# Gated linear attention with a gated feed-forward on one core: the second chunk's phase summed on TensorE, one copy out of PSUM for the turned q and k, and a new order on all engines

## The chip, the core and the metric

The kernel runs on one core of one Trainium2 chip. Its engines are TensorE (PE in the profile; PEld is its weight load), VectorE (DVE), ScalarE (ACT), GpSimd (POOL) and SyncE (SP, which here only starts transfers). Each engine works through its own list of instructions in order, and waits on semaphores where it needs the result of another one. The metric is the device time of the whole program in microseconds, the median of a few runs.

## The reference

Two stages follow one another. The first is a recurrence over 768 tokens for 4 batches of 8 heads with head size 48: a complex state of 48 x 48 per head is multiplied by a complex gate of magnitude below 1 at every token, gains the outer product of k and v, and is read by q. The second is a feed-forward over the 3072 tokens with 384 features.

```python
mag = np.sqrt(a_re * a_re + a_im * a_im)
scale = np.minimum(mag, 0.999) / (mag + 1e-06)
a_re_n, a_im_n = (a_re * scale, a_im * scale)
for t in range(S):                      # S = 768; (B, H, D) = (4, 8, 48)
    new_re = ar * S_re - ai * S_im      # ar, ai: the gate of token t
    new_im = ar * S_im + ai * S_re
    S_re, S_im = (new_re + kv, new_im)  # kv: k outer v of token t
    y[:, :, t] = np.einsum('bhd,bhde->bhe', q[:, :, t], S_re)
# x = y as (3072, 384)
gelu = 0.5 * g * (1.0 + erf(g * inv_sqrt2))       # g = x @ w_gate
ffn_out = gelu * val @ w_out                      # val = x @ w_val, d_ff = 1536
return x + res_gate * ffn_out                     # res_gate = sigmoid(x @ w_res)
```

## The kernel before

**Tiling.** The tokens are cut into 12 groups. Group p holds 256 tokens of batch p % 4 (groups 0 to 3 the first 256 tokens of each batch, 4 to 7 the next, 8 to 11 the last), as two chunks of 128 tokens; a chunk is a tile of 128 tokens by 384 features. The feed-forward runs over 8 units: units 0 to 3 are groups 0 to 3, units 4 to 7 are two groups each.

**Steps.** Every piece of work is a named step; the number is the group or unit, then the chunk or part. For group p:

- Lar, Lai, Lq, Lk, Lvf load a chunk of an input (SP queue). VC casts v.
- SQI, SQR, ADD, LNR, EXR, TH, LM, ATN make the logarithm of the gate's magnitude and its angle (ScalarE and VectorE).
- CSL and CST are TensorE products in float32 with a triangular matrix: they sum the logarithms (line 609) and the angles (line 643) along a chunk's tokens. EX and EI are exponentials of CSL's result. OFF and FR take the whole turns off CST's result; ABS, SIN and COS follow.
- QE, KE (line 705) and QR, KR (line 713) multiply q and k with the magnitude and the turned phase, giving padQ and padK of 96 rows per head.
- q and k are then turned so that the 96 features lie on the partitions. For groups 0 to 4 TensorE does it: TP (line 745) writes 4 heads of q and 4 of k into one PSUM tile of 1024 columns, and two CP steps (line 751) copy 512 columns each to SBUF. For groups 5 to 11 a transposing transfer does it (QT, KT, line 718).
- AT (line 759), AM (762), DK (767), Y (807 and 810), X (818) are attention within the chunk, the causal mask, the state's gain, the output and its copy out of PSUM. EN, EB, MI, ED, and DR, DS, DE, DI, DT, MM, MN bring the state G and its decay from group to group; the D steps are small transfers on POOL's queue.

For unit u: XT and XC, or the transposing transfer XD, turn the attention's output; GP and VP (line 848) are the two up-projections, GE the gelu, HM the product (859), RP and SG the residual gate, OP (873) the down-projection, OT (878), RX (885) and ST the end. The weights (Wg, Wv, Wr, Wo; lines 920 to 926) are loaded with a cast by POOL's queue in 12 pieces; HOLDW and HOLDO are one-element copies on POOL that wait for a given load before later weight pieces are started.

**The carried row.** An angle sum has to go on from chunk to chunk. For groups 4 to 11, after FR of a chunk, CRA (chunk 0 to chunk 1 of the same group) or CRB (chunk 1 to chunk 0 of the next group of that batch), line 688, scales the last 32 rows of the chunk's phase into spare rows of the state tile G, and CDA or CDB (line 693), a transfer that adds, puts its last row onto the first row of the next chunk's angles. CST of the next chunk waits for that. Groups 0 to 3 count chunk 0's angles back from its end and need no carry inside the group.

**What sets the order.** The list ORDER, written out by hand or program, gives all 1,391 steps in one sequence; each engine gets its steps in that sequence. The words log, trig and gelu in it load ScalarE's tables. The dictionary 'eo' says on which engine a step runs where it has a choice. Buffers are taken in turn from rings: four PSUM tiles for CSL, CST, OP, RP, GP, VP, TP and XT, two for AT, one each for Y and DK.

Of the kernel before, what the change touches and what calls it, by code (L numbers as in the profile page):

```python
# [53 lines left out]
 'cpe': ('ACT', 'DVE'),  # L54
# [8 lines left out]
 'cma': [],  # L63
 'xdma': 5,
 'eo': {'CP0.0.0.0': 'ACT',
        'CP0.0.0.1': 'DVE',
        'CP0.0.1.0': 'ACT',
        'CP0.0.1.1': 'DVE',
        'CP0.1.0.0': 'DVE',
        'CP0.1.0.1': 'DVE',  # L70
        'CP0.1.1.0': 'ACT',
        'CP0.1.1.1': 'DVE',
        'CP1.0.0.0': 'DVE',
        'CP1.0.0.1': 'DVE',
        'CP1.0.1.0': 'DVE',
        'CP1.0.1.1': 'ACT',
        'CP1.1.0.0': 'DVE',
        'CP1.1.0.1': 'DVE',
        'CP1.1.1.0': 'ACT',
        'CP1.1.1.1': 'DVE',  # L80
        'CP2.0.0.0': 'ACT',
        'CP2.0.0.1': 'ACT',
        'CP2.0.1.0': 'ACT',
        'CP2.0.1.1': 'DVE',
        'CP2.1.0.0': 'DVE',
        'CP2.1.0.1': 'DVE',
# [24 lines left out]
        'CRA8': 'DVE',
        'CRA9': 'POOL',
        'CRB0': 'DVE',
        'CRB1': 'POOL',
        'CRB2': 'POOL',
        'CRB3': 'POOL',
        'CRB4': 'POOL',
        'CRB5': 'POOL',
        'CRB6': 'DVE',
        'CRB7': 'DVE',  # L120
        'EB10': 'POOL',
# [4 lines left out]
        'EB7': 'POOL',  # L126
        'EB8': 'POOL',
        'EB9': 'ACT',
        'EN10': 'POOL',
# [4 lines left out]
        'EN7': 'POOL',  # L134
        'EN8': 'DVE',
        'EN9': 'POOL',
        'MM10': 'DVE',
# [5 lines left out]
        'MM8': 'POOL',  # L143
        'MM9': 'DVE',
        'MN10': 'POOL',
        'MN11': 'POOL',
        'MN4': 'POOL',
# [4 lines left out]
        'MN9': 'POOL',  # L152
# [12 lines left out]
        'OFF4.0': 'ACT',  # L165
# [3 lines left out]
        'OFF6.0': 'ACT',  # L169
        'OFF6.1': 'DVE',  # L170
# [4 lines left out]
        'OFF9.0': 'ACT',  # L175
        'OFF9.1': 'DVE',
        'RX0.0': 'POOL',
        'RX0.1': 'POOL',
        'RX1.0': 'POOL',
        'RX1.1': 'POOL',  # L180
# [26 lines left out]
        'SQI3': 'DVE',  # L207
        'SQI4': 'DVE',
# [15 lines left out]
        'SQR7': 'DVE',
        'SQR8': 'ACT',
        'SQR9': 'ACT',
        'VC0.0': 'POOL',
        'VC0.1': 'POOL',
        'VC1.0': 'DVE',
        'VC1.1': 'POOL',  # L230
        'VC10.0': 'POOL',
        'VC10.1': 'ACT',
        'VC11.0': 'POOL',
# [3 lines left out]
        'VC3.0': 'POOL',  # L237
# [7 lines left out]
        'VC7.0': 'DVE',  # L245
        'VC7.1': 'POOL',
        'VC8.0': 'POOL',
        'VC8.1': 'ACT',
        'VC9.0': 'ACT',
        'VC9.1': 'POOL',  # L250
        'X0.0': 'ACT',
        'X0.1': 'ACT',
        'X1.0': 'ACT',
        'X1.1': 'ACT',
        'X10.0': 'ACT',
        'X10.1': 'ACT',
# [24 lines left out]
        'XC3.0': 'DVE',
        'XC3.1': 'DVE',
# [6 lines left out]
Lar0.0 log LNR0.0 SQR0.0 Lai0.0 SQI0.0 ADD0.0 LM0.0 Lar0.1 LNR0.1 EXR0.1 Lai0.1 SQI0.1 TH0.1 SQR0.1 EXR0.0 Lai1.1  # L289
CSL0.0 Lai1.0 SQI1 TH0.0 Lar1.0 trig ATN0.1 ADD0.1 Lar1.1 SQR1 ATN0.0 log LM0.1 CST0.0 ADD1 LM1 EX0.0 CST0.1 CSL0.1  # L290
OFF0.0 FR0.0 OFF0.1 Lk0.0 Lvf0.0 Lq0.1 CSL1.1 EI0.0 LNR1 EX0.1 VC0.0 DE0 EXR1 EI0.1 KE0.0 FR0.1 ABS0.1 TH1 trig COS0.1
SIN0.0 ATN1 SIN0.1 CST1.0 CSL1.0 CST1.1 ABS0.0 COS0.0 Lar3.1 Lai4.1 Lai3.0 Lar3.0 Lai3.1 SQR3 SQI3 ADD3 KR0.0 log
EX1.1 LM3 DE1 EI1.0 LNR3 OFF1.0 EX1.0 EI1.1 Lk0.1 Lq0.0 KE0.1 KR0.1 QE0.0 QR0.0 OFF1.1 Lar2.0 Lar4.0 Lar4.1 Lar2.1
Lk1.1 Lai4.0 Lk1.0 Lai2.1 Lai2.0 Lvf0.1 EXR3 Lq1.1 CRB0 FR1.0 FR1.1 Lq1.0 Lvf1.0 TP0.0.1 Lar5.1 CP0.0.1.0 SQR4 ABS1
QE0.1 CP0.0.1.1 AT0.0.1 TP0.0.0 trig COS1 CP0.0.0.0 SQR2 Wg1 SQI4 QR0.1 CP0.0.0.1 SIN1 SQI2 AT0.0.0 TP0.1.1 TH3
AM0.0.0 ADD4 Lai5.1 CP0.1.1.0 ATN3 CP0.1.1.1 DR4 DK0.0 CSL3.0 TP0.1.0 ADD2 VC0.1 CSL3.1 log LNR2 EI3.1 EX3.1 LM2
Lar5.0 AM0.0.1 MI0 Y0.0 KE1 X0.0 EI3.0 LNR4 EX3.0 CP0.1.0.1 CP0.1.0.0 Lai5.0 AT0.1.1 AT0.1.0 EXR2 CST3.0 KR1 AM0.1.1
AM0.1.0 VC1.0 QE1 XT0.0 CSL2.1 Y0.1 CST3.1 EX2.1 OFF3.0 Wv1 EI2.1 QR1 XC0.0 TP1.0.0 TP1.0.1 X0.1 FR3.0 OFF3.1 XT0.1
DK0.1 HOLDO Wg3 Wg0 EXR4 XC0.1 CP1.0.0.1 CP1.0.1.1 GP0.5 FR3.1 ED0 CP1.0.0.0 Lvf1.1 Wr AT1.0.0 GP0.0 GP0.2 HOLDW CRB1
CP1.0.1.0 gelu GE0.5 GE0.2 Wv3 Wg2 TH4 TH2 SQR5 AT1.0.1 RP0.0 TP1.1.1 SG0.0 GE0.0 RP0.1 SG0.1 Wv2 DE3 Wo2 Wv0 VP0.2  # L300
CP1.1.1.0 TP1.1.0 VP0.5 DE2 DK1.0 AM1.0.0 Wo0 AM1.0.1 Y1.0 Wo1 CP1.1.1.1 trig ATN4 AT1.1.1 HM0.5 CP1.1.0.1 Lk2.0 Lk2.1
AM1.1.1 CP1.1.0.0 ATN2 X1.0 GP0.1 GP0.4 CST2.1 HM0.2 GP0.3 AT1.1.0 gelu GE0.1 GE0.3 GE0.4 MI1 SQI5 ABS3 OFF2.1 log LM4
ADD5 CSL2.0 VC1.1 CST2.0 FR2.1 Lq2.1 VP0.4 VP0.3 AM1.1.0 HM0.4 CDB0 DS4.1 HM0.3 Y1.1 Lq2.0 OFF2.0 EI2.0 EX2.0 Lq3.1
Lq3.0 XT1.0 Lk3.0 LNR5 XC1.0 FR2.0 Lk3.1 DR5 CRB3 X1.1 VP0.1 HM0.1 DK1.1 ED1 VP0.0 XT1.1 HM0.0 OP0.1.0 EXR5 XC1.1 TH5
Lar7.1 trig SIN2 OP0.0.0 SIN3 ABS2 COS2 ATN5 GP1.1 COS3 KE2 OT0.1 KR2 QE2 OT0.0 QR2 DS4.0 Lar6.0 gelu GE1.1 RP1.1
GP1.3 SG1.1 GE1.3 GP1.2 TP2.0.0 GE1.2 TP2.0.1 GP1.4 QE3 QR3 CP2.0.0.0 CP2.0.1.1 KE3 CP2.0.1.0 CP2.0.0.1 KR3 CRB2 GE1.4
GP1.5 GE1.5 RP1.0 GP1.0 Lar7.0 SG1.0 AT2.0.1 AT2.0.0 Lvf2.0 Lai6.1 GE1.0 VP1.2 CSL4.0 AM2.0.1 Lar6.1 DS5.0 DS5.1
TP2.1.1 SQR7 log EX4.0 EI4.0 ML4 HM1.2 Lai6.0 ML5 CP2.1.1.0 AM2.0.0 VC2.0 CP2.1.1.1 CSL4.1 VP1.4 VP1.0 HM1.4 HM1.0
TP2.1.0 CP2.1.0.0 CP2.1.0.1 LM5 SQR6 EX4.1 Lvf3.0 Lvf2.1 Lai7.1 Lai7.0 CDB1 RX0.0 DI4 CST4.0 SQI6 Y2.0 CSL5.0 AT2.1.1
OFF4.0 EI4.1 ADD6 FR4.0 EX5.0 LNR6 ME5 EI5.0 Lq4.0 Lk4.0 ST0.0 DK2.0 AT2.1.0 VP1.1 MI2 AM2.1.1 HM1.1 AM2.1.0 VC2.1  # L310
CSL5.1 VP1.5 X2.0 VP1.3 HM1.5 EX5.1 SQI7 EI5.1 DR6 CRA4 HM1.3 ADD7 CST5.0 LM6 EXR6 ME4 OFF5.0 Y2.1 TP3.0.0 CP3.0.0.1
DK2.1 ED2 FR5.0 CP3.0.0.0 TP3.0.1 CP3.0.1.1 TH6 CP3.0.1.0 LNR7 X2.1 OP1.0.0 XT2.0 EXR7 OT1.0 XC2.0 TH7 CDA4 CST4.1
AT3.0.0 OFF4.1 XT2.1 AT3.0.1 TP3.1.1 trig ATN7 ATN6 VC3.0 DT4.1 DK3.0 AM3.0.0 FR4.1 CP3.1.1.1 OP1.1.0 XC2.1 SIN4 MI3
CP3.1.1.0 ABS4 OT1.1 AM3.0.1 GP2.3 GP2.2 TP3.1.0 DT4.0 DR7 RX0.1 COS4 GP2.5 Lvf3.1 CP3.1.0.1 CP3.1.0.0 MM4 CRA5 VC3.1
DK3.1 Y3.0 gelu GE2.5 GE2.3 AT3.1.1 GP2.4 AT3.1.0 RP2.0 RP2.1 GE2.2 GE2.4 Lq4.1 Lk4.1 SG2.1 KE4 AM3.1.1 ED3 KR4 DE5
AM3.1.0 RX1.0 QE4 CDA5 CST5.1 RX1.1 DI5 OFF5.1 SG2.0 MN4 DE4 Lai8.1 GP2.0 X3.0 GP2.1 Lar9.0 Lai9.0 GE2.0 VP2.5 Lvf4.0
Lar8.1 Lq5.1 Lar9.1 FR5.1 VC4.0 DK4.0 QR4 VP2.3 Y3.1 HM2.5 TP4.0.1 TP4.0.0 SQR9 GE2.1 Lvf5.0 VC5.0 DS6.0 HM2.3 trig
SIN5 CP4.0.1.0 CP4.0.1.1 EN4 CDB2 Lai8.0 Lq9.1 CRB5 CP4.0.0.1 Lq6.1 X3.1 CP4.0.0.0 ABS5 Lai9.1 Lar8.0 VP2.0 HM2.0
XT3.0 VP2.2 AT4.0.1 AT4.0.0 XC3.0 AM4.0.1 Lvf4.1 ST1.0 Lvf8.0 VP2.1 VP2.4 CSL6.0 VC8.0 EB4 CRB4 AM4.0.0 COS5 HM2.1
Y4.0 TP4.1.1 Lk8.0 HM2.2 HM2.4 log EI6.0 EX6.0 SQI9 CST6.0 TP4.1.0 Lq5.0 ST1.1 Lk5.0 QE5 ADD9 CP4.1.0.0 LM7 Lk5.1  # L320
CP4.1.0.1 SQR8 SQI8 LNR9 OP2.1.0 CP4.1.1.1 QR5 CP4.1.1.0 OP2.0.0 CDB3 XT3.1 AT4.1.0 OT2.1 OFF6.0 VC4.1 EXR9 ADD8 XC3.1
# [44 lines left out]
class Steps:  # L366
# [24 lines left out]
def kernel(  # L391
# [590 lines left out]
```

## Time and profile before

| | |
|---|---|
| median of 3 runs | 274.76 us (274.43 to 276.25) |
| profiled execution, its own time | 275.13 us |
| its span, first to last instruction | 273.4 us |
| mean granted TensorE clock | 0.963 |
| PE busy | 234.9 us, 86% of the span |
| DVE busy | 222.7 us, 81% |
| ACT busy | 207.9 us, 76% |
| POOL busy | 114.7 us, 42% |
| read from HBM | 31.33 MB |

The profile gives the busy time of each engine, then the same in 40 slices of the span. A group of instructions is told by its source line, engine and tiles, with the count, the summed busy time and the mean of one; the idle time behind it is what the engine lost just before them, with the work that ended the wait. A window answer gives the busy time of each engine between two moments. The difference of 1.7 us between the execution's own time and its span lies around the program's first and last instruction.

### The profile page before, as it was taken

How to read it: one execution, taken by the hardware profiler on the slowest of the kernel's cores; microseconds unless marked ns; L12 is line 12 of the kernel's file. 1: busy time of each engine (PE TensorE's matmuls, PEld its weight loads, DVE VectorE, ACT ScalarE, POOL GpSimd, SP SyncE). 2: the span in 40 equal slices, each digit the busy share in tenths (PEclk: the TensorE clock that was granted, in tenths of full speed). 3: DMA queues.
4: the chain of work that ended last, by engine and by line, in shares of the span. 5: the costliest groups of instructions: out<-in, count | busy, mean ns of one | idle time of the engine just before them, and what ended most of it. 6: DMA issues, size and time to landing. Idle time of an engine off the chain costs nothing.

```text
span 273.4 us, 5330 instructions
## 1 busy us (share of the span) xinstructions
PE 234.9 (86%) x1913; PEld 148.2 (54%) x1926; DVE 222.7 (81%) x369; ACT 207.9 (76%) x343; POOL 114.7 (42%) x164
## 2 busy tenths in 40 slices
PE   0636777978999899997999999899899889999993
PEld 0313546765867777675744565545556445654451
DVE  1888899698999998995899999778998698634534
ACT  5999997999899899797799798979569763124410
POOL 4001197451437798299464385400751250021001
PEclk9985599999999999998999999999999999999999
DMA  7999999999999789899789938697769937132002
GB/s 149 207 207 191 206 199 186 186 183 173 184 220 181 138 181 196 143 174 167 123 166 190 190 70 158 152 215 138 153 74 185 205 80 158 30 95 80 2 29 86
DMA packets 170714, 41.35 MB, mean 151 GB/s; under 512 B 162624, under 2 KB 170688, under 8 KB 170688
## 3 DMA queue, kind: packets, MB, share of 16 engines
q1 hardware_dynamic: 163200, 37.04, 70.1%
q0 software_dynamic: 7488, 3.97, 11.0%
q8 instruction: 15, 0.25, 0.4%
q14 instruction: 11, 0.09, 0.1%
HBM read 31.33 MB, written 4.76 MB: 132 GB/s over the span
## 4 chain that ended last, share of the span: by engine, by line
PE 45%; DMA 18%; ACT 15%; DVE 10%; issue 6%; POOL 3%; SPq 0%; DVEq 0%; ACTq 0%; POOLq 0%
PE gv L848 22%; PE sums L873 8%; DMA wo<-in_moe_w_out_dram 5%; PE sums L643 4%; PE sums L609 4%; DMA wr<-in_moe_w_res_dram 3%; ACT L949 3%; ACT CS L521 3%; DMA KT<-padK 3%; PE sums L863 2%; ACT m L521 2%; DMA xT<-x 2%; PE at L759 2%; DMA QT<-padQ 2%; DVE kE L705 2%
## 5 line engine op out<-in xcount | busy, mean ns | idle before, releaser
L859 DVE SCALAR_TENSOR_TENSOR h<-h,gv 128x512 bf16<-128x512 bf16 x72 | 47.1, 679 | 15.7 <-PE gv L848 15.5
L521 ACT ACTIVATE h<-gv 128x512 bf16<-128x512 f32 x72 | 41.0, 603 | 22.6 <-PE gv L848 21.9
L848 PE MATMUL gv<-xT,wg 128*128 128x256 bf16 (+1 forms) x284 | 52.7, 325 | 4.6 <-DMA xT<-x 1.6
L848 PE MATMUL gv<-xT,wv 128*128 128x256 bf16 (+1 forms) x279 | 55.1, 326 | 1.0 <-DVE h L859 0.6
L873 PE MATMUL sums<-wo,h 128*128 128x384 bf16 x288 | 49.2, 326 | 2.1 <-DMA wo<-in_moe_w_out_dram 1.1
L949 ACT ACT_TABLE_LOAD x34 | 43.6, 1283 | 1.3 <-PEq L966 0.7
L848 PEld LDWEIGHTS <-wg 128*128 128x128 bf16 x288 | 27.4, 98 | 24.0 <-issue 3.8
L873 PEld LDWEIGHTS <-h 128*128 128x128 bf16 x288 | 27.4, 98 | 20.5 <-issue 2.1
L848 PEld LDWEIGHTS <-wv 128*128 128x128 bf16 x288 | 27.2, 99 | 19.0 <-issue 3.8
L762 DVE TENSOR_TENSOR atm<-at,mask 128x512 bf16<-128x512 f32 x48 | 31.8, 681 | 5.5 <-PE at L759 5.2
L885 POOL TENSOR_TENSOR ot<-ot,x 128x384 f32<-128x384 f32 x14 | 14.2, 1019 | 40.0 <-DVE ot L878 39.9
L521 ACT ACTIVATE ar<-ar 128x768 f32<-128x768 f32 (+1 forms) x28 | 23.1, 833 | 0.0
L878 DVE SCALAR_TENSOR_TENSOR ot<-sg,sums 128x384 f32<-128x384 f32 x24 | 12.9, 547 | 10.2 <-PE sums L873 6.3
L532 POOL CAST v<-vf 128x384 bf16<-128x384 f32 x17 | 11.7, 692 | 21.8 <-DMA vf<-in_v_dram 20.7
L609 PE MATMUL sums<-m,lt 128*128 128x384 f32 x24 | 12.3, 600 | 9.0 <-ACT Ei L521 8.5
L643 PE MATMUL sums<-ai,ut 128*128 128x384 f32 x40 | 18.4, 545 | 0.9 <-DMA ai<-G 0.6
L693 POOL DMA_DIRECT2D ai<-G x16 | 14.1, 880 | 8.4 <-ACT ai L521 5.7
L531 ACT CAST x<-y 128x384 bf16<-128x384 f32 x22 | 10.5, 477 | 7.5 <-issue 5.0
L521 ACT ACTIVATE sg<-sums 128x384 f32<-128x384 f32 x24 | 11.7, 499 | 5.1 <-PE sums L863 5.1
L863 PE MATMUL sums<-wr,xT 128*128 128x384 bf16 x72 | 14.6, 325 | 0.6 <-DMA wr<-in_moe_w_res_dram 0.3
L688 POOL TENSOR_SCALAR G<-m 32x384 f32<-32x384 f32 x10 | 14.0, 1397 | 2.8 <-issue 2.1
L521 ACT ACTIVATE m<-m 96x8 f32<-96x8 f32 (+2 forms) x29 | 12.9, 466 | 2.7 <-DMA d<-m 1.1
(94 smaller groups left out, 466.4 us busy)
## 6 DMA issues: line engine op xcount, KB each, us to landing
ar<-in_a_re_dram SPq DMA_DIRECT2D x24, 192.0 KB, 3.8
ai<-in_a_im_dram SPq DMA_DIRECT2D x24, 192.0 KB, 4.0
k<-in_k_dram SPq DMA_DIRECT2D x24, 192.0 KB, 4.3
vf<-in_v_dram SPq DMA_DIRECT2D x24, 192.0 KB, 3.8
q<-in_q_dram SPq DMA_DIRECT2D x24, 192.0 KB, 4.1
out_dram<-ot SPq DMA_DIRECT2D x24, 192.0 KB, 2.5
wg<-in_moe_w_gate_dram POOLq DMA_DIRECT2D x4, 288.0 KB, 7.8
wv<-in_moe_w_val_dram POOLq DMA_DIRECT2D x4, 288.0 KB, 9.2
```

The source lines that it names most:

```text
L521: return nc.scalar.activation(out=out, in_=in_, func=func, **kw)
L609: st.add("CSL%d.%d" % (p, c), "PE", lambda c=c: nc.tensor.matmul(out=st["csl", (p, c)], lhsT=lmat[c], rhs=part(("m2", p), (c,)), start=Tru ...
L643: return r + [nc.tensor.matmul(out=o, lhsT=tmat[c if s == 0 else 1], rhs=part(("ai", p), (c,)), start=not both, stop=True)]
L688: st.add("CR%s%d" % (nm, p), cre, lambda: eng.tensor_scalar(out=row[96:128], in0=part(("m2", p), (c,))[96:128], scalar1=-2.0 * math.pi, sc ...
L693: st.add("CD%s%d" % (nm, p), "POOL", lambda: nc.gpsimd.dma_start(out=part(("ai", pn), (cn,))[0:1], in_=row[127:128], accum_op=OP.add), r=[ ...
L762: st.add("AM" + sfx, "DVE", lambda: nc.vector.tensor_tensor(out=st["atm", i], in0=st["at", i], in1=mask4, op=OP.mult), r=[("at", i)], w=[( ...
L848: st.add("%sP%d.%d" % (nm.upper(), u, f), "PE", lambda f=f, fs=fs, nm=nm, w=w: [nc.tensor.matmul(out=st[nm + "p", (u, f)][:, j * 256:j * 2 ...
L859: st.add("HM%d.%d" % (u, f), "DVE", lambda f=f, h2=h2: nc.vector.scalar_tensor_tensor(out=h2(), in0=h2(), scalar=0.5, in1=gv(("vp", (u, f) ...
L863: st.add("RP%d.%d" % (u, jj), "PE", lambda jj=jj: [nc.tensor.matmul(out=st["rp", (u, jj)], lhsT=st["xT", u][:, i, jj * 128:(jj + 1) * 128] ...
L873: st.add("OP%d.%d.%d" % (u, jj, hh), "PE", lambda jj=jj, fs=fs: [nc.tensor.matmul(out=st["op", (u, jj)], lhsT=st["h2", u][:, f, jj * 128:( ...
L885: st.add("RX%d.%d" % (u, jj), rese, lambda jj=jj, pc=(p, c), eng=eng: eng.tensor_tensor(out=st["ot", (u, jj)], in0=st["ot", (u, jj)], in1= ...
L949: nc.scalar.preload_act_table_set(tables[nm])
```

## The change

Three things are edited, and the order is written anew.

1. For groups 4 to 11, chunk 1 of CST is two products into the same PSUM tile: a matrix that holds 1/(2 pi) everywhere times chunk 0's angles, and the triangular one times chunk 1's. The constant matrix is one column, broadcast. CRA and CDA are gone (8 each); CRB and CDB stay. CST of chunk 1 now reads the angles of both chunks.
2. The two CP copies of 512 columns become one of 1024, on one engine.
3. Every buffer is now picked by a slot number that stands behind the step's name in ORDER, in place of rings.
4. ORDER has 1,355 steps in another sequence, with 34 table loads as before. By the dictionary 'eo', 8 X copies, 3 VC, 4 RX, 4 EB, 3 MN and a few others go to VectorE, and VectorE gives SQI and SQR (one each) to ScalarE; 3 of CRB run on GpSimd where 5 did.

```diff
- 'cma': [],
+ 'cma': [4, 5, 6, 7, 8, 9, 10, 11],
...
-        omat = singles.tile([128, 128], FP, name="omat")
-        nc.vector.memset(omat, I2PI)
+        om = singles.tile([128, 1], FP, name="om")
+        nc.vector.memset(om, I2PI)
+        omat = om.to_broadcast([128, 128])
...
-                for n, eng in enumerate(PARAMS["cpe"]):
-                    eng = on("CP%s.%d" % (sfx, n), eng)
-                    st.add("CP%s.%d" % (sfx, n), eng, lambda n=n, eng=eng: copy(
-                        eng, st["qk", i][0:DD, n * 512:n * 512 + 512], st["tp", i][0:DD, n * 512:n * 512 + 512]),
-                        r=[("tp", i)], w=[("qk", i, n)])
+                cpe = on("CP" + sfx, "DVE")
+                st.add("CP" + sfx, cpe, lambda cpe=cpe: copy(cpe, st["qk", i][0:DD], st["tp", i][0:DD]),
+                       r=[("tp", i)], w=[("qk", i)])
...
-            pools[tag] = ctx.enter_context(tc.tile_pool(name="p" + tag, bufs=PARAMS["bufs"][tag], **kw))
-    psM = ctx.enter_context(tc.tile_pool(name="psM", bufs=4, space=PSUM))
+            pools[tag] = ctx.enter_context(tc.tile_pool(name="p" + tag, bufs=1, **kw))
+    psM = ctx.enter_context(tc.tile_pool(name="psM", bufs=1, space=PSUM))
...
-    tiles["gp"] = tiles["vp"] = lambda: psM.tile([128, 512], FP, name="gv", **mm)
+    tiles["gp"] = tiles["vp"] = lambda sl: psM.tile([128, 512], FP, name="gv", tag="mm" + next(sl))
```

The code that the first edit switches on stood in the kernel before, unused (lines 636 to 645, `both`). The start of the two sequences up to the weights and the first down-projection, most steps left out:

```
before: ... Wg1 SQI4 QR0.1 ... ADD4 Lai5.1 ... DR4 ... Wv1 ... HOLDO Wg3 Wg0 ... GP0.5 ... Wr ... GP0.0 GP0.2 HOLDW CRB1 ... Wv3 Wg2 ... Wv2 DE3 Wo2 Wv0 VP0.2 ... DE2 ... Wo0 ... Wo1 ... HM0.0 OP0.1.0 ... KE2 ... OP0.0.0
after:  ... HOLDO ... ADD4 CP0.0.1 DR4 ... Wg0 Wg2 Wv3 Wg3 ... Wg1 Wv0 ... Wr ... Wo2 Wv1 GP0.5 ... HOLDW ... Wo0 ... DE2 ... VP0.0 ... VP0.5 ... Wv2 ... VP0.4 VP0.2 VP0.3 VP0.1 HM0.2 HM0.3 HM0.1 HM0.4 DS4.0 DR5 Wo1 KE2 ... OP0.0.0
```

More of the change, by code (lines that the diff above doesn't have):

```diff
@@ L125 @@
         'EB6': 'DVE',
[L126 to L129, printed above, removed]
+        'EB7': 'DVE',
+        'EB8': 'DVE',
+        'EB9': 'DVE',
+        'EN10': 'DVE',
         'EN11': 'POOL',
@@ L151 @@
         'MN8': 'POOL',
-        'MN9': 'POOL',
+        'MN9': 'DVE',
         'OFF0.0': 'DVE',
@@ L164 @@
         'OFF3.1': 'DVE',
-        'OFF4.0': 'ACT',
+        'OFF4.0': 'DVE',
         'OFF4.1': 'ACT',
@@ L236 @@
         'VC2.1': 'POOL',
-        'VC3.0': 'POOL',
+        'VC3.0': 'DVE',
         'VC3.1': 'POOL',
@@ L299 @@
[L299 to L308, printed above, removed]
```

365 lines of the change are left out of this document (178 added, 187 removed).

## The prediction

> **What bounds the kernel now.** I read the page's busy slices first, then the PE line of time for its gaps, then the chain of work, then sums over stages.
>
> The page's slices of the span (first line: totals of the engines):
>
> ```profile
> PE 234.9 (86%) x1913; PEld 148.2 (54%) x1926; DVE 222.7 (81%) x369; ACT 207.9 (76%) x343; POOL 114.7 (42%) x164
> ...
> PE   0636777978999899997999999899899889999993
> ...
> DMA  7999999999999789899789938697769937132002
> ```
>
> PE is thin in the first nine slices (some 64 us) and nearly full after. The line of time of PE around that point:
>
> ```profile
> 61.75 0.82 PE L873 MATMUL sums<-wo,h 128*128 128x384 bf16 x4 [0.89 <-DVE h L859]
> 63.64 3.41 PE L873 MATMUL sums<-wo,h 128*128 128x384 bf16 x20 [1.06 <-DMA wo<-in_moe_w_out_dram]
> ```
>
> The first down-projection waits for VectorE, and four products later for the last piece of wo. In the chain of work:
>
> ```profile
> 33.31 0.54 POOL d L594
> 33.85 0.73 POOL v L532
> 34.58 0.71 POOL wv L920
> ...
> 37.67 9.46 DMA wr<-in_moe_w_res_dram
> ...
> 49.40 14.20 DMA wo<-in_moe_w_out_dram
> 63.60 0.04 issue
> 63.64 1.47 PE sums L873 x8
> ```
>
> So before 63.64 us the transfers decide. The window answer over three stages and the tail (columns: stretch, length, busy PE, PEld, DVE, ACT, POOL, clock, DMA share, GB/s):
>
> ```profile
> 0.00:63.64 63.64, 39.16 (x303) 26.45 (x303) 51.81 (x93) 57.36 (x89) 25.79 (x43) 0.87 1.11 190
> 63.64:221.62 157.98, 149.57 (x1293) 96.62 (x1302) 141.97 (x230) 135.82 (x227) 84.44 (x116) 0.99 0.88 162
> 221.62:269.15 47.53, 46.20 (x320) 25.17 (x322) 27.77 (x46) 14.69 (x28) 4.44 (x6) 1.00 0.25 64
> 269.15:273.40 4.25, 0.00 (x0) 0.00 (x0) 1.14 (x3) 0.00 (x0) 0.00 (x0) 1.00 0.37 139
> ```
>
> DMA share 1.11 in the first stage: the transfer engines are full, at 190 GB/s. From 63.64 us to 269.15 us PE is busy 195.8 of 205.5 us; the 94% and 97% leave 9.7 us. The last 4.25 us are OT, RX and the store behind the last product. **The kernel is a start of 63.6 us bound by transfers and VectorE, then 205.5 us of TensorE, then a tail.**
>
> To count TensorE's work I give each step its issue time from the chain of work: GP or VP (6 products of 256 or 3 of 512 columns) 0.65 us, OP 1.95 (12 products), RP 0.49, CSL or one CST product 0.65, TP 0.45, AT 0.225, a pair of products in Y 0.05, DK 0.2 to 0.37. All steps make 228.5 us; 29.0 lie before the first OP and 199.6 from it on. Four products of that OP (0.65) had run by 63.64 us, so 205.5 us carried 199.0 us of work: **6.6 us of loss**, in gaps of 0.2 to 1.7 us that end on many kinds of work, none often.
>
> **The change, part by part.**
>
> *Second phase product.* Eight CST steps become two products. The nearest row is the same shape in float32: "PE sums L643 x2" takes 0.65 us in the chain (one product is two records). 8 x 0.65 = **+5.2 us on TensorE**. The broadcast stationary matrix is not in the trace; the bounds are 0.16 us a product (bf16, 384 columns: 1.95 / 12) and twice 0.65, so +1.3 to +10.4; I take 5.2, since only the weight's access pattern differs. No other work hides it, because all eight products lie after the first OP, where PE has no room.
>
> *The carry.* Away go 8 CRA (5 on POOL at 1.18 us median, 3 on VectorE at 0.36: -5.9 and -1.1) and 8 CDA (0.88 each to issue, 4.1 us to land: -7.0 on POOL). POOL is busy 42% and waits 39.9 us for OT alone, so its time is worth nothing. The chain FR, CRA, CDA, CST loses some 6 us per group, but on PE only one wait of 0.62 us ends on "DMA ai<-G". I take **-0.6 us**; from 0 to -2. What is late next is CST's own input, the angles from ATN.
>
> *One copy.* 29 CP on VectorE at 412 ns and 11 on ScalarE at 578 become 15 and 5. VectorE's 128x384 copy of the same kind takes 348, so 128 columns cost 64 ns and 1024 columns some 0.67 us (between 0.41 and 0.82); ScalarE's 489 and 578 give 0.93 (between 0.58 and 1.16). VectorE 11.95 to 10.0, ScalarE 6.4 to 4.7. AT starts up to 0.35 us later, as two engines no longer share the copy: 7 us over 20 copies at most, 0 to 1 where PE can't do something else. After 63.64 us PE lost 0.32 us on qk: I take 0.
>
> *Engines.* From the 'eo' lists by the rows: X 8 more on VectorE (0.554 each), RX 4 more (0.588), VC 3 (0.436), EB 4 (0.345), MN 3 (0.24), less CP, CRA, SQI, SQR: VectorE **+6.7 us**, ScalarE -5.6, POOL -26. Where does VectorE's surplus fall? Work ahead of the first OP is 61.5 us in the new order against 55.3 (sums of single durations); from there to KR11 it is 158.2 in both; the rest lies in the last 50 us, where VectorE is half idle. So it can only hurt the start. HM0.4, the last that OP0.0.0 needs, has 57 us of VectorE ahead, against 55 for HM0.0 before: ready at about 61.7 + 2 = 63.7 us.
>
> *Weights.* POOL starts them in order. Before, one wg piece goes at 23.1 us, the other 11 from 34.5 us on, all landed at 63.6: 2.65 us a piece while loads of SP share the transfer engines. Now all 12 stand behind DR4, which waits for ADD4. ADD4 has 23.9 us of VectorE ahead against 25.2 (done at 34.2): 33.0 us, plus 0.5 for DR4 is 33.5, and 12 x 2.65 = 31.8: **65.3 us**. Also VP0.4 to VP0.1 now stand behind Wv2, and Wo1 behind DE2, DS4.0 and DR5 in POOL's queue. Bounds: 61 (VectorE alone, if the loads yield) and 69 (two transfers of 4 us ahead). I take 65. SP starts as many loads before the first OP in both (46 and 45), so no bytes go away.
>
> *Order and slots.* Before the first OP of the new order lie 29.6 us of TensorE work, nearly the same 29.0; from it on 204.1 against 199.6. The new order thus puts no added work into the idle start. Its loss after the start is unknown: 0 to 14 us by the rows (6.6 now, twice that); I keep 6.6 less 0.6. Slots fix a buffer but cost no instruction. SP's list holds the same loads and stores; a late XD or QT holds what stands behind it, as now (waits up to 5.5 us there, 1.7 on PE).
>
> **The sum.** 65.0 (start) + 204.1 (TensorE) + 6.0 (loss) + 4.25 (tail) = 279.35 us of span, against 63.6 + 199.0 + 6.6 + 4.25 = 273.4. The execution's own time was 1.73 us above its span: 281.1. The median shown lies 0.37 below that execution: **280.7 us**, 2.2% more.
>
> *A rule beside it.* In the windows of ten microseconds the granted clock is 0.86 from 120 to 130 us and 0.97 in the next ten, around PE's wait of 1.73 us for the turned k, and 0.50 from 20 to 30. The Trainium skill's "TensorE: Matmul & The Clock Gate", section "HAM oscillation", says that idle gaps beyond about 3.4 us bring the half clock back; here a shorter gap preceded it. By that rule a long wait before VP0.4 or OP0.0.0 would add some 1.7 us (half of 3.4, an estimate from that page) and give 282.4.
>
> **Rivals.**
>
> *A. The sum holds* (start 64 to 66, loss 4 to 8): 277.7 to 283.7.
>
> *B. The weights are late.* Place: VP0.4 behind Wv2, OP0.0.0 behind Wo1. For it: SP's loads fill the transfer engines at that moment, DE2 waits for EX2.1, and a small transfer there takes 4 us. Against it: POOL has no CRB in front. With a start of 70 us: 285.7, and 287.4 with a stretch of halved clock like that at 120 us (below 1.00 by 0.14 and 0.03 of ten microseconds: 1.7 us).
>
> *C. The gaps pay for the product.* VectorE gets its two-input operations faster when POOL computes less: kE on line 705 takes 950 ns in the median and 2271 at worst, mean 1146, so 0.2 us a time. (The Trainium skill's "GPSIMD Engine Reference", section "Specifications", says that GpSimd shares its SBUF interfaces with such VectorE operations; this spread agrees.) With a start at 63 us and a loss of 3 us: 274.35 + 1.4 = 275.7; this case spans 272 to 277.5. Against it: PE's gaps seldom end on VectorE.
>
> *D. Faster, the other side.* The start shrinks: with HOLDO early and no work of POOL between the pieces, eight pieces are queued within 7 us of DR4 and the last lands by 59 us; VectorE, freed of POOL, has HM0.4 done by 60.5. It decides if both come before some 61 us. 60.5 + 204.1 + 1.5 + 4.25 = 270.4, or 271.7 by the same offsets. For it: ScalarE has 5.6 us less, and PE's gaps end on varied things. Against it: share 1.11 of the transfer engines, and PE's 204.1 us must run almost without a gap.
>
> *E. The added product is nearly free* (0.16 us each, the lower bound): 276.8; I count it in C.
>
> **Chances and range.** About 1% is what a measurement of this kernel tells from no change (272.0 to 277.5). A 0.50 and B 0.12 are slower: 0.62. C with E 0.18 is the same. D 0.20 is faster. The likeliest is A, 280.7 us. The range reaches over C to the edge of D and over B: 271.5 to 287.5.
>
> **What would show it.** Right: L643 records 48 to 64, PE busy near 240 us; no POOL line for 8 of the adding transfers; PE idle until about 65 us with the wait on wo or wv in front of line 873 or 848 (new numbers), then over 93% busy to the last 4.3 us. Wrong: the first OP before 62 us (D), or a stretch from it to the end with under 3 us lost (C, D), or one broadcast product that issues in under 0.3 us (E). A first OP after 68 us shows B.

## The result, and the profile after

| | before | after |
|---|---|---|
| median of 4 runs | 274.60 us (273.81 to 276.25) | **283.53 us** (282.08 to 284.29) |
| ratio | | 1.0326, 95% interval 1.0284 to 1.0369 |
| profiled execution: own time, span | 275.13, 273.4 us | 283.15, 281.4 us |
| first instruction to the main part of the first down-projection | 63.64 us | 74.36 us |
| from there to TensorE's last product | 205.51 us | 202.79 us |
| tail | 4.25 us | 4.25 us |

A median here and in the later table is over all runs of a kernel, a ratio over the runs within 1.5% of the kernel's fastest.

The change makes the kernel 3.3% slower. The forecast was 280.7 us, in a range of 271.5 to 287.5. By that number it held. By its parts it did not: the start is 10.7 us later than before, where 1.4 were expected, and the stage behind it is 2.7 us *shorter*, where 4.5 more were expected.

The page of the kernel after, totals of the engines and busy tenths of PE and of the transfer engines in 40 slices:

```profile
PE 240.4 (85%) x1931; PEld 151.5 (54%) x1942; DVE 226.5 (81%) x378; ACT 205.3 (73%) x327; POOL 87.4 (31%) x136
...
PE   0537496379889999999998999997999999999993
...
DMA  8999999999939969999999999898785299130112
```

PE has a hole in its eighth and ninth slice (digits 3 and 7, from 49 to 63 us) before it becomes full. The windows by stage (columns: stretch, length, busy PE, PEld, DVE, ACT, POOL, clock, DMA share, GB/s):

```profile
0.00:74.36 74.36, 43.19 (x300) 27.87 (x301) 52.01 (x93) 57.02 (x83) 19.45 (x38) 0.82 1.26 182
74.36:277.15 202.79, 197.24 (x1632) 123.60 (x1641) 173.39 (x284) 148.31 (x245) 67.97 (x98) 1.00 0.79 134
277.15:281.40 4.25, 0.00 (x0) 0.00 (x0) 1.11 (x2) 0.00 (x0) 0.00 (x0) 1.00 0.37 139
```

In the middle stage PE is busy 197.2 of 202.8 us, so 5.6 us are idle; before, it was 195.8 of 205.5, 9.7 idle. All the loss, and more, is in the start. Of the 10.7 us by which it is later, 6.7 are idle time of PE (31.2 us against 24.5) and 4.0 are longer busy time (43.19 against 39.16) for about as many products, at a lower mean clock (0.82 against 0.87). The line of time of PE shows the hole and what ended it:

```profile
57.90 0.58 PE L728 MATMUL tp<-ident,padQ 128*96 128x128 bf16 x4 [6.26 <-ACT h L501]
...
74.36 4.06 PE L854 MATMUL sums<-wo,h 128*128 128x384 bf16 x24
```

PE stood 6.26 us for a GELU of ScalarE (its output is the tile h). The chain of work leads back from there to one load:

```profile
36.13 15.03 DMA ar<-in_a_re_dram
...
51.24 1.58 ACT ar L501 x2
...
57.25 0.61 ACT h L501
57.86 0.04 issue
57.90 1.01 PE tp L728 x8
```

The load of group 5's real part (Lar5.0 in ORDER) was issued at 36.13 us and landed 15.03 us later. SQR5, which squares it, runs on ScalarE in the new order, ahead of the first GELUs; ScalarE works in order, so they stood behind it. The wait in ScalarE's line of time:

```profile
51.24 2.45 ACT L501 ACTIVATE ar<-ar 128x768 f32<-128x768 f32 x3 [5.83 <-DMA ar<-in_a_re_dram]
```

Nine pieces of the weights were started from 34.49 us on and shared the transfer engines with this load, and every load before it had been slow too. The last point is seen in the queues. The DMA part of the page of the kernel before, and then of after (packets, MB, share of 16 engines; then issues, KB each, median us to landing):

```profile
q1 hardware_dynamic: 163200, 37.04, 70.1%
...
ar<-in_a_re_dram SPq DMA_DIRECT2D x24, 192.0 KB, 3.8
ai<-in_a_im_dram SPq DMA_DIRECT2D x24, 192.0 KB, 4.0
```

```profile
q1 hardware_dynamic: 163200, 37.04, 80.2%
...
ar<-in_a_re_dram SPq DMA_DIRECT2D x24, 192.0 KB, 4.7
ai<-in_a_im_dram SPq DMA_DIRECT2D x24, 192.0 KB, 4.5
```

The same 163,200 packets with the same 37.04 MB keep the engines 80.2% busy of a span that is 3% longer, against 70.1%: 22.1 ns a packet against 18.8 (share x 16 x span / packets). From 10 to 30 us little but the loads runs. The q1 queue in that window, before and then after:

```profile
q1 hardware_dynamic: 19728, 3.73, 94.6%
```

```profile
q1 hardware_dynamic: 19726, 3.73, 138.6%
```

That is 15.3 ns a packet before and 22.5 after, and the rate of all queues is 201 GB/s against 187. The share is a sum over packets, and above 100% they overlap. It isn't a few late packets: of those of 192 bytes, the loads, nearly all (99%) take 15 ns before, while after half of them take more than 20 and some up to 38. Nothing in the forecast had said that a packet would take longer. That was the thing to find out.

### The profile page after: what moved, and what is told of

The parts are those of the page before. It is cut to its first block, busy times and chain, and to the rows that moved or that the text cites. A ratio compares the mean times of both kernels' runs of the same rounds, so it can differ in the third digit from the quotient of the medians.

```text
span 281.4 us, 5299 instructions
## 1 busy us (share of the span) xinstructions
PE 240.4 (85%) x1931; PEld 151.5 (54%) x1942; DVE 226.5 (81%) x378; ACT 205.3 (73%) x327; POOL 87.4 (31%) x136
## 3 DMA queue, kind: packets, MB, share of 16 engines
q1 hardware_dynamic: 163200, 37.04, 80.2%
## 4 chain that ended last, share of the span: by engine, by line
PE 59%; DVE 16%; DMA 11%; ACT 6%; issue 4%; SPq 3%; POOL 0%; DVEq 0%; POOLq 0%; ACTq 0%
PE gv L829 26%; PE sums L854 11%; DMA ar<-in_a_re_dram 7%; PE sums L623 5%; PE sums L589 4%; SPq L517 3%; PE sums L844 3%; PE at L740 3%; DVE atm L743 2%; ACT L930 2%; PE sums L622 2%; DVE qE L688 2%; PE tp L728 1%; DMA xT<-x 1%; ACT ar L501 1%
## 5 line engine op out<-in xcount | busy, mean ns | idle before, releaser
L829 PE MATMUL gv<-xT,wg 128*128 128x256 bf16 (+1 forms) x283 | 55.0, 331 | 4.2 <-DVE h L840 1.5
L829 PE MATMUL gv<-xT,wv 128*128 128x256 bf16 (+1 forms) x282 | 54.1, 324 | 1.1 <-DVE qk L512 0.5
L501 ACT ACTIVATE ar<-ar 128x768 f32<-128x768 f32 x29 | 24.1, 842 | 6.5 <-DMA ar<-in_a_re_dram 6.4
L501 ACT ACTIVATE sg<-sums 128x384 f32<-128x384 f32 x24 | 11.7, 491 | 16.0 <-PE sums L844 15.4
L577 POOL DMA_DIRECT2D m<-d x16 | 11.1, 713 | 18.6 <-DMA d<-m 9.4
L623 PE MATMUL sums<-ai,lt 128*128 128x384 f32 x8 | 5.0, 714 | 13.9 <-ACT ai L501 13.9
L728 PE MATMUL tp<-ident,padQ 128*96 128x128 bf16 x80 | 8.5, 234 | 9.6 <-ACT h L501 6.3
L844 PE MATMUL sums<-wr,xT 128*128 128x384 bf16 x72 | 16.0, 342 | 0.0
L512 DVE COPY qk<-tp 96x1024 bf16<-96x1024 bf16 x15 | 10.1, 681 | 7.2 <-PE tp L728 7.2
L696 DVE TENSOR_TENSOR padK<-CS,kE 128x1536 bf16<-128x1536 bf16 (+1 forms) x13 | 13.5, 1043 | 1.2 <-ACT CS L501 1.1
```

The source lines that it names most:

```text
L501: return nc.scalar.activation(out=out, in_=in_, func=func, **kw)
L512: return (nc.vector if eng == "DVE" else nc.gpsimd).tensor_copy(out=out, in_=in_)
L623: return r + [nc.tensor.matmul(out=o, lhsT=tmat[c if s == 0 else 1], rhs=part(("ai", p), (c,)), start=not both, stop=True)]
L696: return nc.vector.tensor_tensor(out=pad, in0=st["CS", p][:, cs[0] * H:(cs[-1] + 1) * H], in1=sb, op=OP.mult)
L728: r.append(nc.tensor.transpose(out=st["tp", i][0:DD, kk + j * 128:kk + j * 128 + 128], in_=f(c * H + hg * 4 + j), identity=ident))
L829: st.add("%sP%d.%d" % (nm.upper(), u, f), "PE", lambda f=f, fs=fs, nm=nm, w=w: [nc.tensor.matmul(out=st[nm + "p", (u, f)][:, j * 256:j * 2 ...
```

## The experiments

In the table, "start" is the moment of the main part of the first down-projection and "rate" that of the windows from 10 to 30 us (both in the profiled execution); the ratio is to the kernel before on the same chip.

| kernel | median us | ratio, 95% interval | start us | rate GB/s |
|---|---|---|---|---|
| before | 273.04 to 274.60, by chip | 1 | 63.64 | 201 |
| after | 283.53 | 1.0326 [1.0284, 1.0369] | 74.36 | 187 |
| before, one copy | 272.96 | 0.9965 [0.9926, 1.0005] | 63.48 | 206 |
| after, square later | 278.57 | 1.0176 [1.0114, 1.0237] | 71.11 | 187 |
| after, without the first product | 279.37 | 1.0234 [1.0171, 1.0297] | 74.28 | 187 |
| before, two products | 275.70 | 1.0102 [1.0043, 1.0161] | 65.08 | 190 |
| after, square later, loads as before | 276.87 | 1.0107 [1.0043, 1.0172] | 71.14 | 187 |
| after, square later, group 1 first | 279.39 | 1.0186 [1.0112, 1.0260] | 71.14 | 187 |
| before, loads as after | 277.06 | 1.0134 [1.0095, 1.0174] | 66.56 | 206 |
| after, tiles on 64 bytes | **272.06** | 0.9937 [0.9899, 0.9975] | 64.53 | 207 |
| after, square later, loads as before, on 64 bytes | 273.28 | 0.9943 [0.9904, 0.9981] | 65.50 | 216 |
| before, two products, on 64 bytes | 272.06 | 0.9951 [0.9920, 0.9981] | 63.74 | 205 |
| before, tiles 32 bytes off | 277.84 | 1.0149 [1.0094, 1.0204] | 64.67 | 190 |
| before, both edits, on 64 bytes | **270.51** | 0.9888 [0.9861, 0.9915] | 64.23 | 204 |

**One copy alone.** The kernel before, with one copy per pair at the place of the first of the two:

```diff
-                for n, eng in enumerate(PARAMS["cpe"]):
-                    ...
+                cpe = on("CP" + sfx, "DVE")
...
- ... Lar5.1 CP0.0.1.0 SQR4 ABS1 QE0.1 CP0.0.1.1 ...
+ ... Lar5.1 CP0.0.1 SQR4 ABS1 QE0.1 ...
```

> The kernel before with the second edit alone: one copy of 1024 columns where two of 512 stood, at the place of the first of the two, on the engines of the changed kernel. Theory: the copies are hidden and cheaper in sum, 274 to 276. Rival (TensorE's score products wait for the longer copy, up to 0.35 us at 20 places): 277 to 281.

It gave 0.9965, with 1 just inside the interval; the 272.96 us lie below both forecasts, which had been set against the 274.6 us of the result (on this chip the kernel before took 273.34). So the copies are hidden or gain a little, and they are no part of the 3.3%.

**The square later.** In the kernel after, SQR5 and ADD5 go behind the GELUs they held up:

```diff
- ... VC1.0:1 Wr SQR5 XT0.0:3 ... DK0.1 ED0 ADD5 VC1.1 ...
+ ... VC1.0:1 Wr XT0.0:3 ... DK0.1 ED0 VC1.1 ... GE0.4 GE0.5 SQR5 AM1.0.0 ADD5 TP1.1.0:00 ...
```

> The changed kernel with two steps put later in the order: the square of group 5's a_re (SQR5, on ScalarE) behind GE0.5, and ADD5 behind AM1.0.0. Theory (the late start is ScalarE standing 5.8 us behind that square for a load that landed 15 us after its start, with the gelus and PE's 6.3 us wait behind it): the wait goes, the first down-projection starts at 67 to 70 us in place of 74.4, time 277 to 279.5. Rival (the loads and weights are late as a whole, whichever step meets them first): the first down-projection stays above 72 us, 281.5 to 284.

The wait of 5.83 us is gone, the start comes 3.3 us earlier, and the time falls from 1.0326 to 1.0176 of before, some 4 us. The time is the theory's; the start, 71.11 us, lies between the two forecasts. Some 7.5 us of late start remain, without one large wait behind them. The square is where the delay was paid, not all of its cause.

**Without the first product.** The kernel after, where the second chunk of groups 4 to 11 leaves out the sum of chunk 0 (so its angles are not the reference's):

```diff
-                 r = [nc.tensor.matmul(out=o, lhsT=omat, ...)] if both else []
+                 r = [nc.tensor.matmul(out=o, lhsT=omat, ...)] if both and False else []
...
-                                              start=not both, stop=True)]
+                                              start=True, stop=True)]
```

> The changed kernel without the eight products of the constant matrix with chunk 0's angles: chunk 1's phases then lack chunk 0's sum; all else as in the changed kernel. Theory (the products stand uncovered on TensorE): 5.2 us less than the changed kernel, 277.5 to 279.5. Rival (the products fill gaps, the loss lies in the start alone): 282 to 284.

279.37 us is just inside the theory's band, but by the ratios, whose intervals overlap, the gain is only 0.9%, about 2.5 us and half of the 5.2. The start is where it was (74.28 us). PE is busy 2.6 us less from there on (194.6 against 197.2), although this execution has a spell of lower clock that the kernel after lacks (0.85 and 0.94 in the two stretches of 8 us from 186.28, an estimated 1.7 us).

**Two products alone.** The kernel before with the first edit of the change, everything else in its old order. The matrix of 128 columns that its unused code would build does not fit beside the other tiles (4.47 KB a partition are left where the last pool needs 4.5), so it has the broadcast column of the kernel after:

```diff
- 'cma': [],
+ 'cma': [4, 5, 6, 7, 8, 9, 10, 11],
...
+        om = singles.tile([128, 1], FP, name="om")
+        nc.vector.memset(om, I2PI)
+        omat = om.to_broadcast([128, 128])
...
- ... DR6 CRA4 HM1.3 ...  TH7 CDA4 CST4.1 ...
+ ... DR6 HM1.3 ...  TH7 CST4.1 ...
```

> The kernel before with only its first edit: the second chunk's phase of groups 4 to 11 is summed by two products (8 more fp32 products of 0.65 us, their lhsT the one broadcast column of the kernel after), and the carried rows and their DMAs are gone; its copies and its order stay. Theory (a product on TensorE costs what is left of it where TensorE is the bound): +2.5 us, which is what leaving the products out of the kernel after gave, to +5.2 us for all eight, so 275.8 to 278.5 us against 273.3. Rival, that the product fills gaps: within 0.7 us of before. Rival, that the carried row's way through POOL and two DMAs was on the path: 2 us or more faster than before.

The time, 275.70 us, came out just under the theory's band. The trace told something else: the loads from 10 to 30 us, none of which the edit touches, ran at 190 GB/s and not at 201. The next three kernels ask whether the order of the loads sets their rate.

**The order of the loads, both ways.** The early loads of after in the order of before (two ways), and those of before in the order of after:

```diff
after, loads as before:
- ... Lai1.1:1 Lar1.1:1 Lai3.0:2 Lai4.1:3 Lai1.0 ... Lar1.0 ... Lk0.0:0 ... Lai3.1 Lvf0.1:0 Lai5.1:4 ... Lar3.1:2 ...
+ ... Lai1.1:1 Lai1.0 Lar1.0:1 Lar1.1 Lk0.0:0 ... Lq0.1:0 ... Lar3.1:2 ... Lai4.1:3 Lvf0.1:0 Lai3.0:2 ...
after, group 1 first:
- ... Lar1.1:1 Lai3.0:2 Lai4.1:3 Lai1.0 ... Lar1.0 ... Lvf1.1:0 Lq0.1 ... Lar5.1:1 Lvf1.0:1 Lar5.0 ...
+ ... Lar1.1:1 Lai1.0 Lar1.0 Lai3.0:2 ... Lai4.1:3 ... Lvf1.1:0 Lvf1.0:1 Lq0.1 ... Lar5.1:1 Lar5.0 ...
before, loads as after:
- Lar0.0 log LNR0.0 SQR0.0 Lai0.0 SQI0.0 ... Lar0.1 LNR0.1 ... Lai1.1 ... Lai1.0 ... Lar1.0 ... Lar1.1 ...
+ Lar0.1 Lai0.1 Lar0.0 ... Lai0.0 ... Lai1.1 ... Lar1.1 Lai3.0 Lai4.1 ... Lai1.0 Lvf0.0 ... Lar1.0 ...
```

> The kernel after with its late square moved as in the run above, and with the early loads (groups 0 to 5) in the order of the kernel before, but for the first four and the loads that take a used buffer. Theory (the late start comes from the order of the loads, which lets group 1 come last and moves 187 GB/s where before moved 203 to 215): 10 to 30 us move at 200 GB/s or more, the first down-projection starts at 64 to 68 us instead of 71.1, and the time is 271.5 to 276 us. Rival (it is the order of the engines' own work): still near 187 GB/s or not, but the first down-projection stays at 70 to 72 us and the time at 277.5 to 279.5 us.

> The kernel after with its late square moved, and three loads moved only: those of group 1's first chunk ahead of groups 3 and 4, and the last v load of group 1 ten loads earlier. Theory (chains that wait for these loads hold up the start): the first square of group 1 starts near 11.3 us instead of 13.3 us, the wait of 12 us behind the v load goes, the first down-projection starts 2 to 4 us earlier than 71.1 us, and the time is 274.5 to 276.5 us; the rate stays near 187 GB/s unless these two neighbours set it. Rival (VectorE's and ScalarE's own work sets the start): within 0.7 us of 278.6 us.

> The kernel before with only its early loads (groups 0 to 5) in the order of the kernel after, but for the loads that take a used buffer. Theory (the order of the loads costs the start): 10 to 30 us move at 190 GB/s or less instead of 203 to 215, the first down-projection starts 4 to 8 us later than 63.6 us, and the time is 277 to 281 us. Rival (order of the engines' work): same rate or not, within 1 us of before's 273.3 us.

The theory that the order sets the rate fell. Both kernels after kept 187 GB/s, and the kernel before ran at 206 GB/s with the order of after. The order does have a price of its own in the kernel before, 1.3% and a start 2.9 us later. In the kernel after, the first of the two moves gained some 0.7% over the late square alone (the intervals overlap) and the second nothing, with the start at 71.14 us in both.

What separates the slow transfers from the fast ones in all these kernels is only whether `om` exists. It is one float a partition, and such a tile is laid out with 32 bytes. All tiles that are allocated behind it, the weights, the state and every loaded buffer, so start 32 bytes higher. No trace shows an address; the count is from the shapes in the kernel. Ahead of the first loaded buffer the kernel before has 55,040 bytes a partition of larger tiles, which is 860 x 64, and two tiles of one float, 64 bytes together. A third one puts all that follows 32 bytes off a multiple of 64. That gave the next theory.

**The address alone.** In the kernel after, and then in two of the kernels above (the kernel after with the square later and the loads as before, and the kernel before with two products), `om` is cut from a tile of 64 bytes; in the kernel before, an unused tile of 32 bytes is put in:

```diff
after, on 64 bytes (and the two others alike):
-        om = singles.tile([128, 1], FP, name="om")
+        om = singles.tile([128, 16], FP, name="om")[:, 0:1]
before, 32 bytes off:
+    sh = singles.tile([128, 1], FP, name="sh")
+    nc.vector.memset(sh, I2PI)
     ident = singles.tile([128, 128], BF, name="ident")
```

> The kernel after with one number changed: the column of the two products is cut from a tile of 16 floats (64 bytes a partition) instead of 1 (which takes 32), so that all tiles behind it start on a multiple of 64 bytes again, as in the kernel before; the computation and the order are the same. Theory (the loads move 187 GB/s instead of 207 because their 192-byte packets land 32 bytes off): 10 to 30 us move at 200 GB/s or more with a DMA share near 1.05 instead of 1.4, the loads land in 3.8 us instead of 4.6, the first down-projection starts at 70 to 72 us instead of 74.4, and the time is 279 to 281.5 us instead of 283.5. Rival (the rate comes from the order or from the missing row transfers): 187 GB/s and within 1 us of 283.

> The kernel before with one unused tile of one float a partition put ahead of the other tiles, which moves all loaded tiles to 32 bytes off a multiple of 64; nothing else is changed. Theory: 187 GB/s and a DMA share near 1.4 in 10 to 30 us, first down-projection 1 to 3 us later than in the kernel before, time 274.5 to 277 us. Rival (the address does not matter): 203 GB/s or more and 273.5 us.

The DMA part of the kernel after on 64 bytes, and then of the kernel before 32 bytes off (each with the q1 queue from 10 to 30 us behind it):

```profile
q1 hardware_dynamic: 163200, 37.04, 68.3%
...
ar<-in_a_re_dram SPq DMA_DIRECT2D x24, 192.0 KB, 4.1
```

```profile
q1 hardware_dynamic: 21912, 4.14, 105.2%
```

```profile
q1 hardware_dynamic: 163200, 37.04, 79.1%
...
ar<-in_a_re_dram SPq DMA_DIRECT2D x24, 192.0 KB, 4.7
```

```profile
q1 hardware_dynamic: 18486, 3.50, 126.8%
```

The whole program has the same packets and bytes in all four; the share of the engines follows the address both ways (80.2% to 68.3%, 70.1% to 79.1%), and so does the landing. From 10 to 30 us a packet takes 15.4 ns in the one and 21.9 ns in the other. The kernel after, with nothing changed but the place of its tiles, is faster than the kernel before: **272.06 us, 0.6% under it, where it was 3.3% over it.** By the two ratios the 32 bytes cost it 3.9%, 10.7 us. They cost the kernel before 1.5%, 4.1 us. Both expectations had the direction and the rate, and both were too small in time: 279 to 281.5 us and 274.5 to 277 were named.

Why so much more in the kernel after shows in the late load again. ScalarE's line of time on 64 bytes, the same square:

```profile
43.95 2.46 ACT L501 ACTIVATE ar<-ar 128x768 f32<-128x768 f32 x3 [2.25 <-DMA ar<-in_a_re_dram]
```

The loads ahead of it go faster, so it is issued at 32.67 us instead of 36.13 and lands by 43.9 instead of 51.2. ScalarE waits 2.25 us instead of 5.83, PE stands 0.50 us at the GELU instead of 6.26, and the first down-projection follows:

```profile
50.62 0.38 PE L728 MATMUL tp<-ident,padQ 128*96 128x128 bf16 x4 [0.50 <-ACT h L501]
...
64.53 4.06 PE L854 MATMUL sums<-wo,h 128*128 128x384 bf16 x24
```

That start is 9.8 us earlier than in the kernel after, out of 10.7. A delay of 3.5 us at the load's issue grew to 7.3 us at its landing. On 64 bytes POOL starts the first pieces of the weights 0.33 us ahead of this load, in the kernel after 1.64 us; that the pieces ahead of it made the difference is argued, not shown.

**The start repaired, and the products, on 64 bytes.** The kernel after with the late square and the loads as before, and the kernel before with two products, both with the wider tile:

```diff
- ... VC1.0:1 Wr SQR5 XT0.0:3 ...
+ ... GE0.4 GE0.5 SQR5 AM1.0.0 ADD5 ...
...
-        om = singles.tile([128, 1], FP, name="om")
+        om = singles.tile([128, 16], FP, name="om")[:, 0:1]
```

> The kernel after with the late square moved, the early loads in the order of the kernel before (both as above) and its tiles on 64 bytes. Theory (late loads make the late start): 200 GB/s or more in 10 to 30 us, the first down-projection at 66 to 69 us instead of 71.1, time 271.5 to 275 us. Rival (past the square, the order of VectorE's and ScalarE's work sets the start): first down-projection still near 71 us, time 276 to 278 us whatever the rate.

> The kernel before with the two products of the second chunk for groups 4 to 11 (as above), and its tiles on 64 bytes. Theory (of the 2.2 us that the products cost with the tiles 32 bytes off, most is the slower loads): 200 GB/s or more in 10 to 30 us, first down-projection at 61 to 62 us instead of 63.3, time 272.5 to 274.5 us, within 0.5% of before. Rival (it is the products): 275 to 277 us.

With its tiles in place, the kernel after gains nothing more from the later square and the other order of loads (0.9943 against 0.9937): what they had repaired was the delay by the address. The two products, which seemed to cost 1.0%, gain 0.5% with the tiles in place. Set against the kernel before with its tiles off as well (1.0149), the 1.0102 is a gain of 0.5% too, though those two intervals overlap: the cost was the address's. Why the products gain is in what PE waits for from the first down-projection on. The table of waits of the kernel before from 64 us on (us in total, times, longest), and then of the kernel before with two products on 64 bytes:

```profile
PE at L759 <- DMA KT<-padK: 1.7, 1, 1.7
PE gv L848 <- DMA xT<-x: 1.6, 2, 1.0
...
PE at L759 <- DMA QT<-padQ: 0.8, 1, 0.8
PE sums L643 <- DMA ai<-G: 0.6, 1, 0.6
```

```profile
PE sums L873 <- DMA wo<-in_moe_w_out_dram: 1.0, 1, 1.0
PE gv L848 <- DVE h L859: 0.7, 1, 0.7
PE gv L848 <- ACT h L521: 0.4, 2, 0.2
PE at L759 <- DVE qk L532: 0.4, 1, 0.4
```

The first row of the second table is the wait that ends at the start, 63.74 us. The 4.7 us in which PE waited for turned k, x and q and for the carried row are gone. From the start to its last product PE is busy 198.3 of 201.5 us there; the idle time fell from 9.7 to 3.3 us, and the stage is 4.0 us shorter (an estimated 1.7 us of it is a spell of lower clock in the kernel before). The start did not move: 63.74 us, where 61 to 62 were expected.

**Both edits in the old order, on 64 bytes.** The kernel before with these lines:

```diff
- 'cma': [],
+ 'cma': [4, 5, 6, 7, 8, 9, 10, 11],
...
+        om = singles.tile([128, 16], FP, name="om")[:, 0:1]
+        nc.vector.memset(om, I2PI)
+        omat = om.to_broadcast([128, 128])
...
+                cpe = on("CP" + sfx, "DVE")
...
- ... Lar5.1 CP0.0.1.0 SQR4 ABS1 QE0.1 CP0.0.1.1 ... DR6 CRA4 HM1.3 ...
+ ... Lar5.1 CP0.0.1 SQR4 ABS1 QE0.1 ... DR6 HM1.3 ...
```

> The kernel before in its own order, with both small edits of the change (the second chunk's phase of groups 4 to 11 by two products; one copy for the turned q and k) and its tiles on 64 bytes. Theory (the two edits gain 0.5% and 0.35% apart, and touch different engines): 270 to 271.5 us, 0.7 to 1% under before, and faster than either edit alone. Rival (both free the same thing, VectorE's time in the same places): 272 us, no better than one of them. Rival (the order of the kernel after is worth more than that of before once its tiles lie on 64 bytes): no faster than 272.1 us, the time of that kernel.

270.51 us, 1.1% under the kernel before: the product of the two ratios alone would be 0.9916, and 0.9888 [0.9861, 0.9915] is at least that. This is the fastest kernel of the study, 0.5% ahead of the kernel after on 64 bytes, with intervals that just overlap.

So of the change's parts the two small edits are worth 1.1% together; the new order with its slots seems to cost about half a per cent (0.9937 against 0.9888, the intervals just overlap); and the 32 bytes of its one new tile cost 3.9% in that order, 1.5% in the old one.

## Why the prediction was right, and where it was wrong

The total was right by luck, because two wrong terms nearly cancelled: the start was forecast 9.4 us too early (65.0 against 74.36), and the stage behind it 7.3 us too long (204.1 + 6.0 = 210.1 against 202.79). The tail was right. 2.1 us of span stayed unforecast, and 2.8 us of the median.

- **"Start 65.0".** This is the step that failed in the kernel after. The forecast counted loads and bytes, found them equal ("no bytes go away"), and took 2.65 us a piece from the kernel before. Bytes and packets are equal indeed; a packet's time is not. The term had been worked out for transfers at the old rate, and where they run at that rate it holds: 64.53 us on 64 bytes. What was missed is a line that the forecast had priced for TensorE alone ("only the weight's access pattern differs"): a new tile also moves what lies behind it.
- **Rival B, "the weights are late".** Its sign came true, a first OP after 68 us, but not its mechanism. PE did not wait for wv or wo at the start; it waited for ScalarE, which waited for a load of SP that shared the transfer engines with the weights. That those engines are full at this moment was rightly named; what came late on them was a load, not a weight.
- **"8 x 0.65 = +5.2 us" for the product.** The size is right. The broadcast product takes as long as the other:

```profile
L622 PE MATMUL sums<-ai,om 128*128 128x384 f32 x16 | 6.8, 507 | 0.0
L623 PE MATMUL sums<-ai,ut 128*128 128x384 f32 x40 | 18.7, 552 | 0.2 <-ACT ai L501 0.2
```

  Two records of some 510 ns run partly side by side; a product issues in 0.65 to 0.77 us in the chain of work, the triangular one mostly in 0.65 to 0.70. From its start on, PE is busy 192.7 us in the kernel before with one copy, and 197.2 with both edits on 64 bytes or 198.3 with the products alone, all at a clock of 1.00: 4.5 to 5.5 us for eight. Rival E (0.16 us each) is out. But in time the products cost only about 2.5 us in the kernel after; the rest went into gaps that PE had.
- **"The carry -0.6".** Mis-sized. The forecast looked for the carried row where PE waits on its last link ("DMA ai<-G", 0.62 us) and bounded it at -2. Three pairs of kernels differ by the first edit (with two copies, with one copy, and with the tiles 32 bytes off). In these PE's waits for the transposes of q, k and x and for the row fell by 3.6 to 4.7 us, and its idle time by 5.5 to 6.4 us; a part of the idle time was filled by the added products. Most of the waits that went are several steps behind the row, at the transposes, which had not been counted as the carry's. That the row's chain, and not its eight small transfers by the room they took, delayed these transposes is argued, not shown; no run parted the two.
- **"One copy 0".** Held on its own: 0.9965, and 681 ns and 1,004 ns a copy where 670 and 930 were estimated. Beside the products it gained more (0.9951 to 0.9888, intervals apart); where that comes from was not looked for.
- **"VectorE +6.7, ScalarE -5.6, POOL -26".** VectorE is busy 226.5 us against 222.7, so +3.8; ScalarE 205.3 against 207.9, -2.6; POOL 87.4 against 114.7, -27.3. The directions hold, the first two sizes are about half. No wait above is traced to them.
- **"Loss 6.0".** PE's idle time in the stage is 5.6 us, so this looks right. But in the kernel before it was 9.7 and not 6.6: it fell by 4.1 us where 0.6 was forecast. And the work term beside it, 204.1 us by issue times, was above the whole stage of 202.79. Work was to grow by 5.1 us (199.0 to 204.1), and PE's busy time grew by 1.5 (195.8 to 197.2); some 1.7 us of that difference is the spell of lower clock in the kernel before (0.86 and 0.97 from 120 to 140 us) that the new kernel lacks, and for the rest summed issue times seem to overstate work that overlaps.
- **Rivals C and D.** With tiles on 64 bytes the time, 272.06 us, comes out at the lower edge of C, with a start at 64.5 us and 4.7 us of idle time. C's mechanism is not seen: kE's mean is 1,155 ns there against 1,146 before, with POOL busy 87.3 us in place of 114.7. Where the products were tried in the old order, it was the lost waits for transposes that paid for them. D's number, 271.7, is near that time, but its mechanism, a start by 61 us, was met in no run.

The rule on the clock stood beside the sum. In the kernel after PE waits 6.26 us up to 57.90, and the granted clock (third number from the end) is about half in the next stretches:

```profile
56.00:60.00 4.00, 2.10 (x13) 1.51 (x13) 1.05 (x2) 3.40 (x6) 0.00 (x0) 0.56 1.27 184
60.00:64.00 4.00, 4.00 (x32) 2.75 (x31) 1.97 (x3) 1.46 (x4) 1.26 (x2) 0.58 1.27 194
```

On 64 bytes, where the wait at that place is 0.50 us, the clock is 1.00 from 52 to 68 us. So the late load cost its wait and then a stretch at about half speed. The Trainium skill's "TensorE: Matmul & The Clock Gate", section "HAM oscillation", says that idle gaps beyond about 3.4 us bring the half clock back. This trace agrees, with its gap of 6.26 us.

The loads read HBM where they did before; what moved is the place that they write to, and a packet took 47% longer (22.5 against 15.3 ns). The Trainium skill's "DMA: Bandwidth & Descriptors", section "How a descriptor splits into AXI transactions", counts extra beats for a read that starts off a multiple of 256 bytes. By that rule alone the loads would have kept their time; the measurement decides.

## What to carry to other kernels

When a change adds a small tile, look at where the tiles behind it now lie: one float a partition moved every loaded buffer off a multiple of 64 bytes and cost 1.5 to 3.9% here, more than any of the edits that were weighed. A sum over bytes needs the rate checked in the same stretch of both traces, packet for packet. And a total that comes out right is no proof of its terms; compare it stage by stage, and price a removed chain by the waits at its far end too.

## What was not expected of the hardware

- Loads in packets of 192 bytes from 10 to 30 us, to buffers 32 bytes off a multiple of 64: 21.9 to 23.5 ns a packet, 187 to 190 GB/s; on a multiple of 64: 15.3 to 15.5 ns, 201 to 216 GB/s. A shift of the same tiles by 64 bytes instead of 32 cost nothing. The busy time of VectorE and ScalarE hardly changes with it (226.5 and 226.8 us, 205.3 and 205.0 in the kernel after), so the engines' own access to these tiles seems indifferent. The weights, whose tiles moved too, came in packets of 768 bytes that took the same time, 78 to 79 ns in the mean both ways. Later in the kernel, where loads are less dense, most packets of 192 bytes take 15 ns even 32 bytes off, so the price seems to need many at once. Whether it lies in the write alone was not tried.
- Where each packet takes 47% longer the rate fell by only 7 to 10%, as more packets overlap (q1's share 1.39 against 0.95 and 1.05). So the rate alone hides most of the effect, and the share shows it.
